# A decay check moved into the boot, a lag of four steps for the second matmuls, and a new order of preparation: an RWKV-6 and tanh-shrink kernel on one Trainium2 core

## The chip, the cores and the metric

The kernel runs on one core of a Trainium2 chip. The metric is the device time of one execution in microseconds; the time before is the median of three runs. The profile was taken from one further execution.

A core has engines that run side by side, each through its own list of instructions in order: TensorE (PE in the profile; its weight loads are PEld), VectorE (DVE), ScalarE (ACT), GpSimd (POOL) and SyncE (SP), which here only starts transfers. An instruction waits for semaphores that others raise. While it waits, all that stands behind it on the same engine waits too. This includes transfers: a transfer that may not yet overwrite its target holds up every later transfer of that queue.

## What is computed

Two layers, one after the other. The first is a linear recurrence (RWKV-6) over 768 tokens, for 4 batches and 8 heads of 48 channels; the second is a dense layer pair with the function h - tanh(h) in between.

```
for t in range(S):
    cur   = einsum(u * k[t], v[t])                  # outer product
    y[t]  = einsum(r[t], state + cur)
    state = w[t] * state + einsum(k[t], v[t])
x = y as (B*S, H*D)                                 # 3072 x 384
h = x @ w_in                                        # 384 -> 2048
out = (h - tanh(h)) @ w_out                         # 2048 -> 384
```

All is float32 on the chip, apart from the two weight matrices, which arrive in 64 bit and are turned into float32 there.

## The kernel before

**Blocks and steps.** The 3072 tokens are cut into 8 blocks of 384 (4 batches, 2 halves `q`). A block's dense part runs in 16 steps `f`, one for each 128 of the 2048 hidden channels. In a step `first` computes `hp`, the first product (3 matmuls of 128x384, six records in the profile, L629); ScalarE copies it to `h` (L632); VectorE and ScalarE make s = h*h (L643), qa (L645), hs and gT (both L635), a short polynomial in place of h - tanh(h), good for small h. Then `Second.add` adds gT times w_out to three accumulators in PSUM (`acc`, L676, again six records). `hp` has a single PSUM buffer, so the next hp waits for the copy to h. The tile `s` of step f is made in step f; qa, hs and gT of step f stand one step later in the program (`rest`). The second matmuls of step f come LAG steps after its hp; LAG is 3, and the pool of gT tiles has LAG + 1 buffers.

**The next block's attention between the steps.** While block i runs its 16 steps, the attention of block i + 1 is made in between, by the plan of `plan(i)`: `before` names what VectorE and ScalarE prepare in step f, `phases` what PE does, `ahead` what is begun for block i + 2, and `loads` which transfer is asked for. The pieces, for pairs of heads (`h1` = pairs 2 and 3, `h2` = pairs 0 and 1, in chunks of 64 tokens):

- `behind`: a scan from the right over the decays w, product of the decays after each token, into the tile `post` (L300, 128x780). `inverse`: the whole product of each chunk and its reciprocal, into `start` (L321, L323). `before`: the scan from the left into `pre` (L289). Both scans read the tile `w`.
- `times_behind`: post = k * post (L314). `times_before`: pre = r * pre (L307). `times_u`: k = u * k on ScalarE (L328).
- `turn`: transposes of post on PE (L386) and a copy `ks` (L388). `update`: k v products (L405) and the states of the chunks (L417, L428), which stay in SBUF.
- `own` and `earlier`: two products of a chunk with itself on PE (L363), taken into the tile `scores` under a mask on VectorE (L370).
- `from_states` (L469) and `from_scores` (L486): the result, copied into xT and `late` by ScalarE (L519). x has 384 rows in three tiles xT; each pair of heads leaves two holes of 16 rows in its tile, filled from the tile `late` by six small transfers (`fill_holes`, L526).
- `bound`: one ScalarE instruction (L334) that sums relu(w - 1) over the block's decays into `excess`, a check that no decay is above 1. At the very end all checks are counted, and if one fails, all is computed again by another path; with this input none fails.

The tiles w, k, r, post, pre and v_sb have one buffer each. So the load of block i + 2's w, asked for while block i runs, may start only when the last reader of block i + 1's w is done.

**The order is written out by hand.** PE, VectorE, ScalarE and SyncE run in program order. A load of the plan is tied by `begin_behind` to the ScalarE instruction that makes h in that step. Within a step the program has, in this order: hp and h, s, the rest of the step before, the weight conversion for step f + 2 (`extra`), the pieces of `before`, the phase, `ahead`, the load, the second matmuls of the lagging step, and, where the phase is "result 1", the "result 2" with its copies and hole fills.

**The boot.** Before block 0's steps, `boot` makes block 0's attention alone, with PE, VectorE and ScalarE waiting on each other, starts the weight loads and converts the first weights. Conversion of one step's weights (`convert`) takes three ScalarE instructions (L205, L208, L209) and two VectorE instructions (L212, L213) over 1536 columns in all. During block 0 the remaining weights are converted as well (step f makes those for f + 3). Only block 0 has this work.

For block 0 the plan has `w` of block 2 in step 11, `k` in 12, `r` in 13, "result 1" in 13 and `bound` of block 1 in 14.

Of the kernel before, what the change touches and what calls it, by code (L numbers as in the profile page):

```python
# [37 lines left out]
F32 = mybir.dt.float32  # L38
# [3 lines left out]
BF16 = mybir.dt.bfloat16  # L42
# [3 lines left out]
AF = mybir.ActivationFunctionType  # L46
# [5 lines left out]
P = 128  # L52
L = 64
NB = 384
NQ = S // NB
NCH = NB // L
NCP = NCH // 2
NPAIR = H // 2
# [12 lines left out]
BANK = 512  # L71
AHEAD = 6
RAWS = 5
LAG = 3

# [21 lines left out]
def kernel(  # L97
# [86 lines left out]


    blocks_n = B * NQ
    n_whole, n_excess, n_top = blocks_n * NPAIR * NCH, blocks_n, blocks_n * NF
# [11 lines left out]
    def convert(f, raw, _, halves=False):  # L199


        lo, hi = raw[:, :, 0], raw[:, :, 1]
        a = w_sb[:, f, :].bitcast(I32)
        up = conv.tile([P, 2 * DM], I32, name="up", tag="up", bufs=4)
        nc.scalar.activation(out=a.bitcast(F32), in_=hi.bitcast(F32), func=AF.Copy, scale=HIGH_SCALE)  # L205
        low, high = (up.bitcast(t).rearrange("p (n two) -> p n two", two=2)[:, :, i]
                     for i, t in enumerate((U16, F16)))
        nc.scalar.activation(out=high, in_=hi.bitcast(F32), func=AF.Copy, scale=SIGN_SCALE)  # L208
        nc.scalar.activation(out=low, in_=lo.bitcast(U32), func=AF.Copy, scale=2.0 ** -29)  # L209

        def part(at):
            return [lambda: nc.vector.tensor_single_scalar(a[:, at], a[:, at], 3, op=ALU.logical_shift_left),  # L212
                    lambda: nc.vector.tensor_tensor(out=a[:, at], in0=a[:, at], in1=up[:, at], op=ALU.add)]  # L213
# [10 lines left out]
    class Block:  # L224
# [102 lines left out]
                t = self.tokens("k", p, 1)  # L327
                nc.scalar.activation(out=t, in_=t, func=AF.Copy, scale=u_sb[:, p:p + 1])  # L328

        def bound(self):  # L330

            i = self.b * NQ + self.q
            junk = work.tile([P, WIDE], BF16, name="junk", tag="junk", bufs=1)
            nc.scalar.activation(out=junk, in_=self.tile("w")[:, 0:WIDE], func=AF.Relu, bias=shift[:, 3:4],  # L334
                                 accum_out=excess[:, i:i + 1])

        def held(self, p0, n):
            i = (self.b * NQ + self.q) * NPAIR * NCH
# [136 lines left out]

        def from_scores(self, yp, slots, first, last):
            for n, slot in slots:
                for p in slot:
                    for c in range(NCP):
                        for h in range(2):  # L480
                            for par in range(2):
                                toks = slice(64 * par, 64 * par + 64)
                                e0 = 64 * (h ^ (p % 2))
                                f0 = p * D2 + h * D
                                n0 = (n * NCP + c) * L
                                nc.tensor.matmul(yp[p % 2][e0:e0 + D, par, n0:n0 + L],  # L486
                                                 lhsT=self.v[toks, c, f0:f0 + D],
                                                 rhs=A[toks, h, p, c, :],
                                                 start=(first and n == slots[0][0] and c == 0),
                                                 stop=(last and (n, c) == (slots[-1][0], NCP - 1)),  # L490
                                                 skip_group_check=True)
# [58 lines left out]
        def prepare(self, name):  # L550
            what, *half = name.split()
            p0, n = (int(half[0]), UP) if half else (0, NPAIR)
            getattr(self, what)(*(() if what == "bound" else (p0, n)))

        def totals(self, m, p0, n):
            cols = slice(p0 * NB, (p0 + n) * NB)
            tot = self.tile("w")[:, cols] if m == 1 else self.tots[m]
            t2 = tot.rearrange("d (n two) -> d n two", two=2)  # L560
            nxt = dense.tile([P, NB], F32, name="tot", bufs=3, tag={1: "h", 2: "s", 4: "qa"}.get(m, "tot"))
# [64 lines left out]
    def first(xT, f, ps):  # L626
        hp = ps.tile([P, NB], F32, name="hp", tag="hp")
        for kc in reversed(range(KC)):
            nc.tensor.matmul(hp, lhsT=w_in_sb[:, f, kc, :], rhs=xT[kc],  # L629
                             start=(kc == KC - 1), stop=(kc == 0))  # L630
        h = dense.tile([P, NB], F32, name="h", tag="h")
        return h, nc.scalar.activation(out=h, in_=hp, func=AF.Copy, scale=1.0 / UPSCALE)  # L632

    def product(out, in0, scalar, in1, op0):
# [50 lines left out]
    def plan(i):  # L685


        ahead = {13: ("behind 2", "inverse 2"), 14: ("behind 0", "inverse 0")}
        if i == 0:
            phases = {6: "turn", 8: "own", 9: "update", 11: "earlier", 13: "result 1"}  # L690
            before = {0: ("behind 0", "inverse 0"), 1: ("before 2",), 2: ("before 0",),
                      3: ("times_behind 2",), 4: ("times_behind 0", "times_u 2"),
                      5: ("times_before", "held", "times_u 0"), 14: ("bound",)}
            converted = range(READY, NF)
            loads = {f: "weights" for f in (0, 1, 2, 4, 5, 6, 7, 8, 9, 10)}
            loads.update({3: "v", 11: "w", 12: "k", 13: "r"})
        else:
            phases = {4: "turn", 5: "own", 6: "update", 8: "earlier", 10: "result 1"}
            before = {0: ("before 2",), 1: ("before 0",), 2: ("times_behind 2", "times_behind 0"),
                      3: ("times_before", "held", "times_u 2"), 4: ("times_u 0",), 7: ("bound",)}  # L700
# [21 lines left out]
    def boot(ps, blk, later):  # L722
        h1, h2 = HALVES
        for p0 in HALVES:
            for name in ("w", "k", "r"):
                blk.load(name, p0, UP)
        blk.load_v()
        for _ in range(3):
            more_weights(nc.sync)
        ready = []  # L730

        def converted():
            for op in ready.pop(0):
                op()

        both = (h1, h1 + 1), (h2, h2 + 1)

        def decays(p0):
            blk.behind(p0, UP)
            blk.inverse(p0, UP)  # L740
            blk.times_behind(p0, UP)
            blk.times_u(p0, UP)
            blk.turn(ps, p0)
            return blk.before(p0, UP)

        decays(h1)
        own = blk.own(ps, h1)
        blk.times_before(h1, UP)
        earlier = blk.earlier(ps, h1)
        blk.bound()  # L750
        ins = decays(h2)
        begin_behind(ins, later.load("w"))
        own()
        blk.update_1(ps)
        blk.times_before(h2, UP)
        earlier()
        ready.append(convert(*raws.pop(0), halves=True))
        blk.results(ps)
        blk.result("from_scores", both[0])
        blk.update_2()  # L760
        blk.result("from_states", ALL, cs=(0, 1), more=True)
        own = blk.own(ps, h2)
        blk.result("from_states", ALL, cs=(2,))
        own()
        earlier = blk.earlier(ps, h2)
        earlier()
        ready.append(convert(*raws.pop(0)))
        blk.result_out(both[0], True)
# [141 lines left out]
```

## Time and profile before

| | |
|---|---|
| time, median of 3 runs | 620.99 us (620.25 to 622.24) |
| profiled span | 617.5 us |
| PE busy | 585.7 us, 95% |
| PE weight loads busy | 362.7 us, 59% |
| VectorE busy | 378.3 us, 61% |
| ScalarE busy | 235.6 us, 38% |
| boot, until the first hp | 28.11 us |
| one middle block, 16 steps | 72.1 us |
| `bound`, each of 8 | 1583 ns, and 190 ns to read its sum |
| transfers | 43.03 MB, mean 70 GB/s |

The page cuts the span into 40 slices of 15.4 us; a digit is the busy share of a slice in tenths. The chain of waits follows the work that ended last back to what released it, piece by piece with start and length. A row of a group or of the timeline has start, length, engine, line, operation, output and inputs, shapes, count, and in brackets how long the engine had been idle and what ended that. A queue of an engine (SPq) is its sequencer, which starts the transfers.

### The profile page before, as it was taken

The page shows a single profiled execution, that of the slowest core. Times are in us where ns is not written, and L with a number is a line of the kernel's source. Part 1 is how long each engine was busy: PE and PEld are TensorE (multiplying, and loading weights), DVE is VectorE, ACT ScalarE, POOL GpSimd, SP SyncE. Part 2 cuts the span into 40 slices and gives each one's busy share as a digit, 9 for nine tenths or more (in the row PEclk, how much of TensorE's full clock was granted, in tenths as well). Part 3 has the DMA queues.
Part 4 walks back from the last instruction along what each step waited for, and adds up shares of the span by engine and source line. Part 5 has one row for each costly group of instructions (what it writes and reads, how often), then busy time and mean ns, then how long its engine had stood idle before and what let it go on. Part 6 is the DMA issues. An engine that isn't in the chain of part 4 may idle for free.

```text
span 617.5 us, 12779 instructions
## 1 busy us (share of the span) xinstructions
PE 585.7 (95%) x5410; PEld 362.7 (59%) x5410; DVE 378.3 (61%) x777; ACT 235.6 (38%) x428; POOL 9.9 (2%) x39
## 2 busy tenths in 40 slices
PE   3779996999999999999999999999999999999996
PEld 3535663566655666566655666556665666555553
DVE  8899992766368553776457663685537764444442
ACT  3789773242224333242233422243332522332221
POOL 5000000000000000000000000000000000000000
PEclk9999999899999999999999999999999999999999
DMA  8594414111212032020321112120320200001001
GB/s 313 169 373 154 155 54 164 40 37 54 63 52 78 1 103 63 1 77 2 105 62 38 39 54 63 51 77 1 104 63 1 76 2 2 11 0 40 0 0 41
DMA packets 23420, 43.03 MB, mean 70 GB/s; under 512 B 2112, under 2 KB 21312, under 8 KB 23360
## 3 DMA queue, kind: packets, MB, share of 16 engines
q1 hardware_dynamic: 22944, 41.89, 20.3%
q8 instruction: 43, 0.70, 0.5%
q10 hardware_dynamic: 352, 0.25, 0.1%
q14 instruction: 17, 0.14, 0.1%
q0 software_dynamic: 64, 0.05, 0.0%
HBM read 36.28 MB, written 4.72 MB: 66 GB/s over the span
## 4 chain that ended last, share of the span: by engine, by line
PE 89%; DVE 6%; issue 1%; DMA 1%; POOL 1%; ACT 0%; SPq 0%; PEld 0%; PEldq 0%; DVEq 0%; POOLq 0%
PE acc L676 39%; PE hp L629 39%; PE att L363 4%; PE att L469 2%; PE att L486 2%; PE att L405 2%; PE att L386 1%; DVE pre L289 1%; DMA xT<-late 1%; DVE w_sb L213 1%; DVE post L300 1%; POOL mask_all L144 1%; DVE scores L370 0%; DVE gT L635 0%; DVE w_sb L212 0%
## 5 line engine op out<-in xcount | busy, mean ns | idle before, releaser
L629 PE MATMUL hp<-xT,w_sb 128*128 128x384 f32 x768 | 273.7, 493 | 13.0 <-DMA xT<-late 6.4
L676 PE MATMUL acc<-w_sb,gT 128*128 128x384 f32 x768 | 271.5, 490 | 0.8
L629 PEld LDWEIGHTS hp<-xT,w_sb 128*128 128x128 f32 x768 | 146.2, 192 | 117.0 <-issue 14.1
L676 PEld LDWEIGHTS acc<-w_sb,gT 128*128 128x128 f32 x768 | 143.3, 190 | 95.7 <-issue 2.5
L643 DVE CUSTOM_DVE_ANT_0 s<-h 128x384 f32<-128x384 f32 x128 | 71.1, 556 | 193.5 <-ACT h L632 193.2
L632 ACT ACTIVATE h<-hp 128x384 f32<-128x384 f32 x128 | 62.8, 491 | 322.3 <-issue 288.5
L635 DVE SCALAR_TENSOR_TENSOR gT<-qa,hs 128x384 f32<-128x384 f32 x128 | 71.5, 558 | 16.7 <-PE acc L676 0.5
L645 ACT ACTIVATE qa<-s,shift 128x384 f32<-128x384 f32 x128 | 77.6, 606 | 5.6 <-DVE top L643 5.4
L635 DVE SCALAR_TENSOR_TENSOR hs<-h,s 128x384 f32<-128x384 f32 x128 | 70.9, 554 | 0.0
L300 DVE TENSOR_TENSOR_SCAN post<-w,seed 128x780 f32<-128x780 f32 x16 | 28.5, 1784 | 10.9 <-DMA w<-in_wT 10.9
L370 DVE COPY_PREDICATED scores<-mask_all,att 128x768 f32<-128x768 uint8 x32 | 30.6, 1004 | 0.8 <-PE att L363 0.6
L289 DVE TENSOR_TENSOR_SCAN pre<-w,start 128x780 f32<-128x780 f32 x16 | 28.5, 1784 | 0.0
L386 PE MATMUL att<-ident,post 128*128 128x128 f32 x96 | 13.4, 292 | 10.0 <-DVE post L314 10.0
L328 ACT ACTIVATE k<-k,u_sb 128x384 f32<-128x384 f32 x32 | 17.7, 604 | 7.5 <-DVE post L314 7.5
L386 PEld LDWEIGHTS att<-ident,post 128*128 128x128 f32 x96 | 11.9, 151 | 12.4 <-DVE post L314 10.2
L208 ACT ACTIVATE up<-raw 128x768 f16<-128x768 f32 x16 | 17.0, 1066 | 0.0
L209 ACT ACTIVATE up<-raw 128x768 uint16<-128x768 uint32 x16 | 16.8, 1050 | 0.0
L519 ACT COPY late<-att 128x384 f32<-128x384 f32 (+1 forms) x9 | 4.3, 478 | 31.5 <-PE att L486 30.5
L213 DVE CUSTOM_DVE_ANT_0 w_sb<-w_sb,up 128x1536 uint16<-128x1536 uint16 (+1 forms) x17 | 15.5, 911 | 0.8
L428 DVE TENSOR_TENSOR states<-states,att 128x192 f32<-128x192 f32 x40 | 14.2, 354 | 2.2
L363 PEld LDWEIGHTS att<-r,k 48*64 48x64 f32 x768 | 12.7, 140 | 4.7 <-issue 4.4
L405 PEld LDWEIGHTS att<-v_sb,ks 64*64 64x64 f32 x704 | 12.8, 143 | 4.2 <-issue 3.8
(52 smaller groups left out, 255.6 us busy)
## 6 DMA issues: line engine op xcount, KB each, us to landing
raw<-in_weights SPq DMA_DIRECT2D x16, 768.0 KB, 5.5
w<-in_wT SPq DMA_DIRECT2D x7, 780.0 KB, 4.6
k<-in_kT SPq DMA_DIRECT2D x7, 768.0 KB, 5.6
r<-in_rT SPq DMA_DIRECT2D x7, 768.0 KB, 4.7
v_sb<-in_v SPq DMA_DIRECT2D x8, 576.0 KB, 3.9
out_y<-o SPq DMA_DIRECT2D x23, 192.0 KB, 1.9
xT<-late SPq DMA_DIRECT2D x44, 24.0 KB, 1.9
w<-in_wT SPq DMA_DIRECT2D x2, 390.0 KB, 4.8
```

The source lines that it names most:

```text
L289: return nc.vector.tensor_tensor_scan(out=self.tile("pre")[:, cols], data0=self.tile("w")[:, cols], data1=start[:, cols], initial=0.0, op0 ...
L300: return nc.vector.tensor_tensor_scan(out=back(t[:, 0:width]), data0=back(self.tile("w")[:, a:a + width]), data1=back(seed[:, a:a + width] ...
L363: nc.tensor.matmul(dst, lhsT=self.chunk(lhs, p, 2 * c + par)[rows], rhs=src, start=True, stop=True)
L370: return lambda: nc.vector.copy_predicated(out=A[:, :, p0:p0 + UP].rearrange("s h p c t -> s h (p c) t"), mask=mask.to_broadcast([P, 2, UP ...
L386: nc.tensor.transpose(tp[:, p, c * P:(c + 1) * P], self.chunk("post", p0 + p, 2 * c, n=2), ident)
L405: nc.tensor.matmul(kvp[64 * h:64 * h + 64, par, n0:n0 + D], lhsT=ks[toks, p % UP, c, 64 * h:64 * h + 64], rhs=self.v[toks, c, e0:e0 + D], ...
L629: nc.tensor.matmul(hp, lhsT=w_in_sb[:, f, kc, :], rhs=xT[kc], start=(kc == KC - 1), stop=(kc == 0))
L632: return h, nc.scalar.activation(out=h, in_=hp, func=AF.Copy, scale=1.0 / UPSCALE)
L635: return lambda: nc.vector.scalar_tensor_tensor(out=out, in0=in0, scalar=scalar, in1=in1, op0=op0, op1=ALU.mult)
L643: nc.vector.tensor_tensor_reduce(out=s, in0=h, in1=h, scale=1.0, scalar=0.0, op0=ALU.mult, op1=ALU.max, accum_out=top[:, n:n + 1])
L645: return g, [lambda: nc.scalar.activation(out=qa, in_=s, func=AF.Square, bias=shift[:, 4:5]), product(hs, h, TOP, s, ALU.mult), product(g, ...
L676: nc.tensor.matmul(acc, lhsT=g[:, j * P:(j + 1) * P], rhs=w_out_sb[:, f, :], start=(f == 0), stop=(f == NF - 1))
```

## The change

Four things, all in the order of work; no arithmetic changes.

1. `bound` now runs for half of the heads at a time (`excess` has two columns per block). Block 1's two halves move from step 14 of block 0 into the boot; the blocks after run both in step 7 as before.
2. LAG is 4: gT has five buffers, h has four, and each step's second matmuls come one step later.
3. Block 0's steps prepare block 1 in another order: the left scans, needed only by "earlier" in step 11, move to steps 4 and 6, the products with k move forward to 1 and 2, "turn" from 6 to 5.
4. In the boot the left scan of h1 comes ahead of the product with k, `own` of h2 is computed and masked ahead of the state updates, `earlier` of h2 stands between two parts of `from_states`, and `from_scores` goes through a pair of heads in reverse, as the copies after it do.

The aim is to have the tile w free before block 2's load is asked for, to take work that is not yet needed out of the stretch in which VectorE is behind, and to fill waits of the boot.

```
-LAG = 3
+LAG = 4
...
-        def bound(self):
-            i = self.b * NQ + self.q
-            junk = work.tile([P, WIDE], BF16, ...)
-            nc.scalar.activation(out=junk, in_=self.tile("w")[:, 0:WIDE], ...)
+        def bound(self, p0):
+            i = 2 * (self.b * NQ + self.q) + p0 // UP
+            junk = work.tile([P, UP * NCH * LP], BF16, ...)
+            nc.scalar.activation(out=junk, in_=self.tile("w")[:, p0 * NCH * LP:(p0 + UP) * NCH * LP], ...)
...
         def from_scores(self, yp, slots, first, last):
             for n, slot in slots:
-                for p in slot:
+                for p in reversed(slot):
...
-        h = dense.tile([P, NB], F32, name="h", tag="h")
+        h = dense.tile([P, NB], F32, name="h", tag="h", bufs=4)
...
         if i == 0:
-            phases = {6: "turn", 8: "own", 9: "update", 11: "earlier", 13: "result 1"}
-            before = {0: ("behind 0", "inverse 0"), 1: ("before 2",), 2: ("before 0",),
-                      3: ("times_behind 2",), 4: ("times_behind 0", "times_u 2"),
-                      5: ("times_before", "held", "times_u 0"), 14: ("bound",)}
+            phases = {5: "turn", 8: "own", 9: "update", 11: "earlier", 13: "result 1"}
+            before = {0: ("behind 0", "inverse 0"), 1: ("times_behind 2",), 2: ("times_behind 0",),
+                      4: ("before 2",), 5: ("times_u 2",), 6: ("before 0", "times_u 0"),
+                      7: ("times_before", "held")}
...
     def boot(ps, blk, later):
-        decays(h1)            # behind, inverse, times_behind, times_u, turn, before
+        blk.behind(h1, UP)
+        blk.inverse(h1, UP)
+        blk.before(h1, UP)
+        blk.times_behind(h1, UP)
+        blk.times_u(h1, UP)
+        blk.turn(ps, h1)
         own = blk.own(ps, h1)
         blk.times_before(h1, UP)
         earlier = blk.earlier(ps, h1)
-        blk.bound()
-        ins = decays(h2)
+        blk.bound(h1)
+        blk.bound(h2)
+        ...                   # behind, inverse, times_behind, times_u, turn of h2
+        ins = blk.before(h2, UP)
         begin_behind(ins, later.load("w"))
         own()
-        blk.update_1(ps)
+        own = blk.own(ps, h2)
         blk.times_before(h2, UP)
         earlier()
+        blk.update_1(ps)
+        own()
         ready.append(convert(*raws.pop(0), halves=True))
         blk.results(ps)
         blk.result("from_scores", both[0])
         blk.update_2()
+        ready.append(convert(*raws.pop(0)))
+        later.bound(h1)
         blk.result("from_states", ALL, cs=(0, 1), more=True)
-        own = blk.own(ps, h2)
+        earlier = blk.earlier(ps, h2)
         blk.result("from_states", ALL, cs=(2,))
-        own()
-        earlier = blk.earlier(ps, h2)
         earlier()
-        ready.append(convert(*raws.pop(0)))
         blk.result_out(both[0], True)
+        later.bound(h2)
         blk.fill_holes([nc.sync, nc.scalar, nc.gpsimd])
```

More of the change, by code (lines that the diff above doesn't have):

```diff
@@ L186 @@
     blocks_n = B * NQ
-    n_whole, n_excess, n_top = blocks_n * NPAIR * NCH, blocks_n, blocks_n * NF
+    n_whole, n_excess, n_top = blocks_n * NPAIR * NCH, 2 * blocks_n, blocks_n * NF
     holds = const.tile([P, n_whole + n_excess + n_top], F32, name="holds", tag="holds")
@@ L328, in times_u @@
                 nc.scalar.activation(out=t, in_=t, func=AF.Copy, scale=u_sb[:, p:p + 1])
-        def bound(self):
-            i = self.b * NQ + self.q
-            junk = work.tile([P, WIDE], BF16, name="junk", tag="junk", bufs=1)
-            nc.scalar.activation(out=junk, in_=self.tile("w")[:, 0:WIDE], func=AF.Relu, bias=shift[:, 3:4],
-                                 accum_out=excess[:, i:i + 1])
+        def bound(self, p0):
+            i = 2 * (self.b * NQ + self.q) + p0 // UP
+            junk = work.tile([P, UP * NCH * LP], BF16, name="junk", tag="junk", bufs=1)
+            nc.scalar.activation(out=junk, in_=self.tile("w")[:, p0 * NCH * LP:(p0 + UP) * NCH * LP], func=AF.Relu,
+                                 bias=shift[:, 3:4], accum_out=excess[:, i:i + 1])
         def held(self, p0, n):
@@ L552, in prepare @@
             p0, n = (int(half[0]), UP) if half else (0, NPAIR)
-            getattr(self, what)(*(() if what == "bound" else (p0, n)))
+            getattr(self, what)(*((p0,) if what == "bound" else (p0, n)))
         def totals(self, m, p0, n):
@@ L560, in totals @@
             t2 = tot.rearrange("d (n two) -> d n two", two=2)
-            nxt = dense.tile([P, NB], F32, name="tot", bufs=3, tag={1: "h", 2: "s", 4: "qa"}.get(m, "tot"))
+            nxt = dense.tile([P, NB], F32, name="tot", bufs=4 if m == 1 else 3, tag={1: "h", 2: "s", 4: "qa"}.get(m, "tot"))
             nxt = nxt[:, 0:n * NB // (2 * m)]
@@ L699, in plan @@
             before = {0: ("before 2",), 1: ("before 0",), 2: ("times_behind 2", "times_behind 0"),
-                      3: ("times_before", "held", "times_u 2"), 4: ("times_u 0",), 7: ("bound",)}
+                      3: ("times_before", "held", "times_u 2"), 4: ("times_u 0",), 7: ("bound 2", "bound 0")}
             converted = ()
@@ L736, in boot @@
         both = (h1, h1 + 1), (h2, h2 + 1)
[L738 to L744, printed above, removed]
-        decays(h1)
+        blk.behind(h1, UP)
[4 more added lines that the diff above has]
+        blk.turn(ps, h1)
         own = blk.own(ps, h1)
@@ L749, in boot @@
         earlier = blk.earlier(ps, h1)
-        blk.bound()
-        ins = decays(h2)
+        blk.bound(h1)
+        blk.bound(h2)
+        blk.behind(h2, UP)
+        blk.inverse(h2, UP)
+        blk.times_behind(h2, UP)
+        blk.times_u(h2, UP)
+        blk.turn(ps, h2)
+        ins = blk.before(h2, UP)
         begin_behind(ins, later.load("w"))
         own()
-        blk.update_1(ps)
+        own = blk.own(ps, h2)
         blk.times_before(h2, UP)
         earlier()
+        blk.update_1(ps)
+        own()
         ready.append(convert(*raws.pop(0), halves=True))
```

## The prediction

> **What bounds the kernel now.** First the slices of the page.
>
> ```profile
> PE   3779996999999999999999999999999999999996
> ...
> DVE  8899992766368553776457663685537764444442
> ...
> PEclk9999999899999999999999999999999999999999
> ```
>
> PE is full except in slices 1 to 3 (to 46 us), in slice 7 (93 to 108 us) and in the last. The only dip of the clock is beside the dip in slice 7. Then the busy time by stage: stretch, length, and busy us of PE, PEld, DVE, ACT, POOL with instruction counts, then granted clock, DMA share and GB/s.
>
> ```profile
> 28.10:49.50 21.40, 16.43 (x42) 8.34 (x43) 20.63 (x36) 18.17 (x25) 0.00 (x0) 0.92 0.87 315
> 49.50:102.60 53.10, 52.95 (x608) 33.12 (x608) 40.52 (x79) 39.28 (x59) 0.13 (x2) 1.00 0.32 111
> 102.60:115.20 12.60, 6.27 (x13) 3.61 (x14) 8.53 (x18) 1.61 (x3) 0.00 (x0) 0.73 0.45 158
> 115.20:187.30 72.10, 71.99 (x686) 44.70 (x685) 43.48 (x91) 23.77 (x47) 0.13 (x2) 1.00 0.17 53
> ```
>
> From 28 to 49.5 VectorE is the bound (20.63 of 21.40 us). From 49.5 PE is, without a gap, and from 115.2 every block takes 72.10 us with 71.99 of PE: nothing there to win. What is left is the boot (28 us), the VectorE stretch, and a hole at the change from block 0 to block 1. The chain of waits says what makes the hole.
>
> ```profile
> 96.78 1.08 PE acc L676 x4
> 97.85 1.58 ACT junk L334 x2
> ...
> 99.45 0.38 SPq L274
> ...
> 100.99 0.80 SPq L526
> 101.78 0.04 issue
> 101.83 6.97 DMA xT<-late
> 108.80 0.14 issue
> 108.93 4.18 PE hp L629 x6
> 113.11 2.11 PE acc L676 x6
> ```
>
> SyncE's queue runs in order. The w load of block 2 (plan step 11) must overwrite the tile that `bound` of block 1 (step 14, L334) still reads. So w, k and r, and behind them the six hole fills (L526), start only when `bound` ends. The list of waits of that queue has the size:
>
> ```profile
> SPq L274 <- ACT junk L334: 22.5, 1, 22.5
> ```
>
> The fills need only the copies of block 1's result, which began at 94.72, yet they go out from 100.99, behind 2.3 MB. PE ends its last matmul at 102.58 and waits until 108.93, 6.35 us; the six matmul records of the next hp then take 4.18 us, where they take 1.94 elsewhere.
>
> **What the Trainium skill says.** "TensorE: Matmul & The Clock Gate", Part 1: after an idle window of about 3.4 us the PE clock is halved until it has been busy about as long. The trace agrees: 6.35 us idle, then 4.18 for 1.94. "DMA: Bandwidth & Descriptors", Issuing engines are not separate DMA queues: all transfers share the same 16 engines. The trace agrees: the fills beside the loads took up to 7.6 us to land, 1.8 to 1.9 elsewhere. "ScalarE: Activation LUTs", What ACT_TABLE_LOAD costs: with a pointer bias 280 ns + 0.833 ns per column, for 1560 columns an estimate of 1.58 us; the trace has 1583 ns.
>
> **The change, part by part.**
>
> *1. `bound` of block 1 into the boot.* The remaining readers of block 1's w tile are the scans; the last ("before 0") now stands at step 6, about 59 us. The w load then goes at step 11 (h at 79.88), k at 12, r at 13 (89.37), each by its own trigger, apart by 4 to 5 us, about their median time to land (4.6 to 5.6). When the copies come at 94.72 the queue is empty. Six fills take 3.98 us to issue (4.08 in the next block) and 1.9 to land: 95.2 + 4.0 + 1.9 = 101.1, before PE asks at 102.6, and xT[2], asked first, is filled first. So 6.35 us of waiting and 4.18 - 1.94 = 2.24 of slow clock go: **-8.6**. All of it is on PE's path, since PE is full before and after. VectorE's own wait for w (10.9 us ahead of L300) goes too, hidden by the lag.
>
> *2. `bound` in two halves.* Per half the price above gives 0.93 us for 780 columns, plus the 0.19 of the accumulator read. In blocks 2 to 7 that adds some 0.5 us to ScalarE, which is busy 23.8 of 72.1: nothing.
>
> *3. Preparation by need.* Between w_sb[3] (ends 39.8) and w_sb[5] VectorE gives up two L289 scans (next start 1.69 us later) and takes two L314 products (0.86): 0.83 us earlier for w_sb[4], 1.66 for w_sb[5]. These are what hp waits for:
>
> ```profile
> 44.55 1.78 DVE L289 TENSOR_TENSOR_SCAN pre<-w,start 128x780 f32<-128x780 f32 x1
> ...
> 44.78 2.17 PE L629 MATMUL hp<-xT,w_sb 128*128 128x384 f32 x6 [0.64 <-DVE w_sb L213]
> ...
> 49.52 2.17 PE L629 MATMUL hp<-xT,w_sb 128*128 128x384 f32 x6 [0.64 <-DVE w_sb L213]
> ```
>
> *4. The lag of four.* It puts every hp one acc group (1.94 us) earlier in PE's order, so while PE waits for weights it has less to do meanwhile. With 3: hp[4] at 44.78 - 0.83 = 43.95. Behind it only acc[0], then hp[5] at 43.95 + 2.01 + 1.94 = 47.90, when w_sb[5] is just there (49.52 - 1.66 = 47.86). From there PE is full, but one acc group is still owed that the old order had behind it: 47.90 + 1.94 = 49.84 against 49.52, less 0.07 of restart: **+0.25**. The two parts nearly cancel.
>
> Does PE stay full to step 16? Times on the old clock. ScalarE at steps 5 and 6 does 5.92 and 4.56 us (h, qa, three conversions, k times u, ks) while PE does 5.2 and 3.9: h[7] ends near 60.95, and hp[8], which needs its PSUM buffer, is due at 60.9, a tie. VectorE has w_sb[12] (behind the eleven state updates, 4.3 us) at 81.45, hp[12] is due at 81.65, slack 0.2. Other weights have 0.9 us or more. I take 0 to 0.5 lost, middle 0.1. The extra gT and h buffers only make the lag possible.
>
> *5. The boot.* VectorE: the L289 scan ahead of the first L314 product fills the 0.49 us for which that waited on GpSimd. The mask of own(h2) ahead of the state updates takes away the 0.65 us before the last mask. With the small waits beside them, placing each row after the one before it has the last mask done at 23.85, not 25.36. But ScalarE does not keep up. earlier(h2) now stands ahead of from_states of pair 2 on PE, where its PSUM buffer comes free only with the fourth state update, so the result copies start at 23.4 (23.14 before), and last 1.96 us to 25.35. Then `bound` of the later block's second half (0.93 + 0.19, less overlap: 1.0) is queued ahead of the two xT copies: 26.4 against 26.47 before. Behind those are VectorE's xT copies (each waits for ScalarE's) and then hp[0]: about 28.0 against 28.11. The reversed from_scores lets the first copy go half a group (0.45 us) sooner, hidden by that `bound`. Bounds: 0 (ScalarE as worked out) and 1.6 (0.49 + 0.65 + 0.45, if it does not bind). I take **-0.1**: the copies and `bound` are one after the other on one engine, with durations from rows.
>
> *6. Blocks 1 to 7 and the end.* PE order shifts, its sum does not. At the end four acc groups are left, not three; two still stand between the last hp and the check, the same 0.51 us of PE waiting there: nothing.
>
> Sum: -8.6 + 0.25 + 0.1 - 0.1 = -8.35, so 620.99 - 8.35 = **612.6 us**.
>
> **The rivals.**
> *A, the boot pays too* (0.10): the half `bound` fits beside the copies, and the 1.6 comes through: 611.1. For it: VectorE's queue holds two waits that the order removes. Against: the ScalarE sum above.
> *B, a new stall follows the lag* (0.12): hp[12] or hp[8] is late by 0.5 us more, or the gap ahead of hp[4] (about 1.75 us, with no acc group behind hp[3] now) halves the clock for one group, 2.24: 612.6 + 2.7 = 615.3. For it: slack of 0.2 us. Against: a gap of 2.3 us ahead of hp[3] left the clock full.
> *C, the fills stay late* (0.05): r, asked for at step 13, is still moving at 95, and six small fills creep beside it; half the hole stays, clock included: 617.
> *D, slower* (0.03): w is held by something else that is as late (the trace shows only the last releaser), so the hole stays whole; the lag's loss of 0.25 and one slow group of 2.24 come on top: 620.99 + 0.25 + 2.24 = 623.5. Against: no other reader of that tile stands later than step 6.
> The forecast itself: 0.70.
>
> **How the numbers follow.** The time is that of the forecast. Low end 610.3: A less the spread of the measured runs (0.75 below their median). High end 615.6: B, with 0.3 for measuring. Outside lie C, D and the tails of A and B, some 0.16. Faster by over 0.3% (below 619.1): forecast, A, B, C, 0.95 with a little taken off for causes not seen; within: 0.02; slower: 0.03.
>
> **What would show it.** In the chain after the change, block 1's first hp follows an acc group with no DMA piece, and the six records take 1.94 or so, with the clock at full in slice 7. The fills land in about 2 us. The w load of step 11 waits for h, not for L334. The first hp starts near 28, the idle ahead of hp[5] is gone, the idle ahead of hp[4] grows to about 1.75. I am wrong if a wait for xT or for w_sb appears on PE after 48 us, if ScalarE's L334 does not stand between the copies of the boot, or if a block from 115 on takes other than 72.1 us.

## The result, and the profile after

The changed kernel takes **614.81 us** (median of 4 runs, 614.09 to 615.3) against 620.62 us (4 runs, 619.19 to 622.24) for the kernel before: a ratio of 0.9905, 95% interval 0.9877 to 0.9932. Run again later beside eleven runs of before it took 614.47 us, ratio 0.9882 (0.9858 to 0.9906). So it is 6 to 7 us faster. The forecast was 612.6 us: the direction and the cause hold, and some 2 us of the gain are missing. Executions of one kernel differ by up to 3.5 us (e1 below: 611.04 to 614.55), so a profile, which shows one of them, can lie that far from a median.

The slices of the page after, the same three rows as before:

```profile
PE   3669899999999999999999999999999999999996
...
DVE  8798986855377644766367563786447663444442
...
PEclk9999899999999999999999999999999999999999
```

The hole of slice 7 is gone, and the dip of the clock with it. In its place there is an 8 in slice 5 (61 to 77 us), in PE and in PEclk. Busy time by stage, after (stretch, length, busy us of PE, PEld, DVE, ACT, POOL with counts, clock, DMA share, GB/s):

```profile
28.76:49.07 20.31, 14.42 (x37) 7.05 (x37) 19.08 (x36) 17.06 (x25) 0.00 (x0) 0.92 0.87 327
49.07:98.00 48.93, 47.24 (x586) 29.70 (x586) 44.02 (x81) 36.10 (x53) 0.13 (x2) 0.97 0.47 162
98.00:111.50 13.50, 13.50 (x43) 7.99 (x42) 8.59 (x18) 4.06 (x9) 0.00 (x0) 1.00 0.05 13
111.50:183.60 72.10, 71.99 (x685) 44.73 (x684) 43.63 (x91) 24.03 (x49) 0.13 (x2) 1.00 0.17 53
```

The change from block 0 to block 1 (third row) is solid: 13.50 of 13.50 us. A later block takes 72.10 us with 71.99 of PE, to the digit what it took before. But the second row has lost 1.69 us of PE time and runs at a clock of 0.97, where before it had 52.95 of 53.10 at 1.00. The chain of waits over the change of block has no transfer in it any more (start, length, what); block 1's first hp is the piece at 105.66:

```profile
97.72 2.13 PE hp L629 x6
99.86 1.94 PE acc L676 x6
101.79 1.94 PE hp L629 x6
103.73 1.94 PE acc L676 x6
105.66 1.94 PE hp L629 x6
```

SyncE's queue in that stretch, after: w, k and r wait for h only, no longer for `bound`; the fills go out at 98.34.

```profile
SPq L274 <- ACT h L632: 12.1, 3, 5.2
```

Where the second row lost its time is in PE's timeline, after (start, length, engine, line, what, idle time and releaser in brackets):

```profile
41.18 2.17 PE L629 MATMUL hp<-xT,w_sb 128*128 128x384 f32 x6 [2.73 <-DVE w_sb L213]
45.12 2.17 PE L629 MATMUL hp<-xT,w_sb 128*128 128x384 f32 x6 [1.77 <-DVE w_sb L213]
...
49.07 2.17 PE L629 MATMUL hp<-xT,w_sb 128*128 128x384 f32 x6
...
67.99 2.10 PE L629 MATMUL hp<-xT,w_sb 128*128 128x384 f32 x6
71.63 1.61 PE L405 MATMUL att<-v_sb,ks 64*64 64x48 f32 x80 [1.55 <-DVE scores L370]
73.17 3.90 PE L676 MATMUL acc<-w_sb,gT 128*128 128x384 f32 x6
```

The rows at 45.12 and 49.07 are as forecast (1.77 us of idle ahead of hp[4], none ahead of hp[5]). The last two are new: `update` waits 1.55 us for the masks of `own`, and the acc group behind it runs at half speed, 3.90 us for the 2.2 that it takes elsewhere. `update` writes its products into the scratch tiles of PSUM (pool ps_a, two buffers), and those two hold the two `own` products until VectorE has masked them into `scores`. VectorE's row of that masking, after and then before:

```profile
70.56 1.94 DVE L370 COPY_PREDICATED scores<-mask_all,att 128x768 f32<-128x768 uint8 x2
```

```profile
68.52 1.91 DVE L370 COPY_PREDICATED scores<-mask_all,att 128x768 f32<-128x768 uint8 x2
```

Before, the masks came 2 us sooner (0.65 us of that because the first hp did, 28.11 against 28.76) and `update` ran without a wait behind the hp of 68.22. VectorE does the same 69 instructions between the boot and the masks in both orders, 42.4 us of work, without a break of note before. After, it stands idle for 0.61 us in a weight conversion and for 0.98 us at step 6: there it is ahead of ScalarE, which has the copies of `turn` (L388) to do before it makes h. ScalarE and VectorE, after:

```profile
55.81 1.48 ACT L388 COPY ks<-att 128x768 f32<-128x768 f32 x2
57.18 0.51 ACT L632 ACTIVATE h<-hp 128x384 f32<-128x384 f32 x1
```

```profile
57.72 0.56 DVE L643 CUSTOM_DVE_ANT_0 s<-h 128x384 f32<-128x384 f32 x1 [0.98 <-ACT h L632]
```

The second left scan (60.83) and the product with r (65.60) are still ahead of the masks at that time.

The difference of the two profiled spans, 617.5 - 613.6 = 3.9 us, is less than that of the medians, because the profiled execution of before (619.19 us) was one of its shortest: its other executions in this study had spans of up to 622.4 us, mostly around 619.

### The profile page after: what moved, and what is told of

It reads as the page before. It is cut to its first block, busy times and chain, and to the rows that moved or that the text cites. A ratio compares the mean times of both kernels' runs of the same rounds, so it can differ in the third digit from the quotient of the medians.

```text
span 613.6 us, 12671 instructions
## 1 busy us (share of the span) xinstructions
PE 584.2 (95%) x5410; PEld 361.6 (59%) x5410; DVE 378.2 (62%) x777; ACT 237.5 (39%) x444; POOL 11.4 (2%) x39
## 4 chain that ended last, share of the span: by engine, by line
PE 87%; DVE 6%; ACT 2%; issue 1%; POOL 1%; PEld 0%; ACTq 0%; PEldq 0%; DVEq 0%; POOLq 0%
PE acc L676 39%; PE hp L629 38%; PE att L363 3%; PE att L469 2%; PE att L405 2%; PE att L486 2%; PE att L386 1%; DVE w_sb L213 1%; POOL mask_all L144 1%; DVE post L300 1%; DVE gT L635 1%; DVE w_sb L212 1%; DVE pre L289 1%; DVE s L643 1%; DVE hs L635 1%
## 5 line engine op out<-in xcount | busy, mean ns | idle before, releaser
L405 PE MATMUL att<-v_sb,ks 64*64 64x48 f32 x704 | 13.4, 220 | 2.6 <-DVE scores L370 2.2
```

Source lines behind the costliest of these rows:

```text
L405: nc.tensor.matmul(kvp[64 * h:64 * h + 64, par, n0:n0 + D], lhsT=ks[toks, p % UP, c, 64 * h:64 * h + 64], rhs=self.v[toks, c, e0:e0 + D], ...
```

## The experiments

In what follows "the pass" is `bound` of block 1, and "order by need" the new order of preparation. There were twelve runs, e8 and e11 repeats among them, each in rounds with the kernel before on the same chip. The median of before differs between the chips by up to 0.6 us (620.72 to 621.35), so the ratios are what is to be compared; e1 to e4 shared a chip, e5 to e8 another, e9 to e11 a third, and e12 had one of its own.

| kernel | median us | ratio to before, 95% |
|---|---|---|
| pass at step 9, nothing else (e1) | 612.14 | 0.9871 (0.9851 to 0.9892) |
| the same again (e11) | 611.86 | 0.9854 (0.9836 to 0.9873) |
| the change, pass back at step 14 (e2) | 623.92 | 1.0049 (1.0032 to 1.0066) |
| the change with lag 3 (e3) | 611.56 | 0.9856 (0.9842 to 0.987) |
| the change, update at step 10 (e4) | 615.57 | 0.9915 (0.9901 to 0.9928) |
| the change, pass at step 9 (e5) | 613.99 | 0.9884 (0.9859 to 0.9909) |
| e5 with the boot of before (e6) | 613.85 | 0.9879 (0.9855 to 0.9903) |
| e5 with lag 3, a left scan and the product with r later (e7) | 612.33 | 0.9853 (0.9825 to 0.988) |
| the change again (e8) | 614.47 | 0.9882 (0.9858 to 0.9906) |
| before, hole fills from ScalarE's queue (e9) | 620.16 | 0.9992 (0.998 to 1.0004) |
| e6 with lag 3 (e10) | 611.87 | 0.9857 (0.9839 to 0.9876) |
| e1 with lag 4, halves (e12) | 613.49 | 0.987 (0.9854 to 0.9887) |

### Is the hole the whole gain? e1, e11 and e2

e1, on the kernel before:

```
-                      5: ("times_before", "held", "times_u 0"), 14: ("bound",)}
+                      5: ("times_before", "held", "times_u 0"), 9: ("bound",)}
```

> The kernel before with one edit: bound of block 1, whole, at step 9 of block 0 instead of step 14; boot, lag and order of preparation as before. Theory (the gain is the hole at the change from block 0 to block 1, and the other three parts together cost some 2.5 to 4 us): the wait for xT and the slow hp after it go, -8.6 us, so about 612.0, some 3 us under the changed kernel; first hp at 28.1 and no wait of PE between 49.5 and 102.6. Rival (the other parts carry a share of the gain, or hide what the early load collides with): 615 or more, with a wait left on PE before step 16 or for xT.

Measured: 612.14 us, ratio 0.9871, and 611.86, 0.9854 on another chip. One moved name takes away 8.0 to 9.1 us (0.0129 and 0.0146 of 621); the medians say 8.7 and 8.9. In e1's profile SyncE's queue sends w at 81.00, k at 86.63, r at 90.50 and the fills from 96.22, and PE runs on through the change of block:

```profile
101.09 2.10 PE L676 MATMUL acc<-w_sb,gT 128*128 128x384 f32 x6
103.02 2.10 PE L629 MATMUL hp<-xT,w_sb 128*128 128x384 f32 x6
```

> The kernel before with the pass over block 1's decays whole at step 9 instead of step 14, run again on the chip of the two others, as their yardstick: 611.0 to 612.5 us by the theory; 614 us or more if its first time was luck of the chip's clock.

e2, the other side, on the changed kernel:

```
-                      7: ("times_before", "held")}
+                      7: ("times_before", "held"), 14: ("bound 2", "bound 0")}
...
-        later.bound(h1)
-        later.bound(h2)
```

> The changed kernel with block 1's two bound halves back at step 14 of block 0, out of the boot. Theory: the hole is back in full, 6.4 us idle and 2.2 of slow clock, less about 1.0 us that the boot gains because no bound stands between its copies: 614.8 + 8.6 - 1.0 = 622.4. Rival (lag, order and boot have a gain of their own): 620 or less.

Measured: 623.92 us, ratio 1.0049. The hole is back, as PE's timeline of this kernel shows:

```profile
110.82 3.54 PE L629 MATMUL hp<-xT,w_sb 128*128 128x384 f32 x5 [6.51 <-DMA xT<-late]
```

The time is 1.5 us above the 622.4 expected: the 1.0 us that the boot was to gain did not show. So the earlier pass is the whole gain, and **the rest of the change costs 3.0 us** (0.0049 of 621; 2.0 to 4.1 by the interval). Both together fit the changed kernel: 0.9854 to 0.9871 times 1.0049 is 0.990 to 0.992, measured 0.9905 and 0.9882.

### Is the queue's order the whole of the hole? e9

```
-                self.fill_holes([nc.sync])
+                self.fill_holes([nc.scalar if self.b + self.q == 1 and self.b == 0 else nc.sync])
```

> The kernel before, with one edit: the six fills of block 1's decay inputs, which stand behind the wait for the w load on SyncE's queue, are issued from ScalarE's queue instead. The pass over the decays stays at step 14. Theory (the queue's order made the hole, and the pass itself is still a chain of its own): the fills go out near 95 us and the 6.5 us wait ahead of block 1's first preparation product goes, but VectorE still waits some 10 us for w, until about 104, so that its masks come late and TensorE waits some 3 us at a later update or accumulation: 615.5 to 617.5 us. Rival (the lag of three steps hides VectorE's wait, the hole was the queue's order alone): 612 to 613 us, no wait of TensorE above 1 us between 90 and 115. Second rival (the fills were held by the bound itself, not by the queue): 620 to 621 us, the hole stays.

(The six fills are not decay inputs: they fill the holes of x, for block 1's first hp.) Measured: 620.16 us, ratio 0.9992: no gain that can be told. That is the time which the second rival named, but not for its reason: the fills did go early and landed in 1.9 us, and block 1's first hp came at 104.21 without a wait. PE waited at other places instead. ScalarE, VectorE and PE in this kernel:

```profile
96.42 3.17 ACTq L526 DMA_DIRECT2D xT<-late  x5
```

```profile
106.94 1.78 DVE L300 TENSOR_TENSOR_SCAN post<-w,seed 128x780 f32<-128x780 f32 x1 [13.59 <-DMA w<-in_wT]
```

```profile
100.24 2.20 PE L629 MATMUL hp<-xT,w_sb 128*128 128x384 f32 x6 [1.27 <-ACT h L632]
...
104.21 2.10 PE L629 MATMUL hp<-xT,w_sb 128*128 128x384 f32 x6
110.82 4.21 PE L676 MATMUL acc<-w_sb,gT 128*128 128x384 f32 x6 [4.51 <-DVE gT L635]
```

Issuing the fills holds ScalarE's queue for 3.17 us, so that h and with it `bound` come later; w comes later still, and VectorE stands before its scan for 13.59 us with s, hs and gT of the dense part behind it in the queue. PE waits 1.27 us for h and 4.51 for gT, and the slow clock after that takes 2.1 more: 7.9 us together, nearly the 8.6 of the hole. The wait behind the wait is there, as the first theory said, but its size was under-estimated (615.5 to 617.5 expected), in part since the cost of issuing on ScalarE was left out: w went out at 102.29, before at 99.45. What helps is to let w go early, not to take the fills past it.

### Which part of the rest costs? e3, e5, e6, e8

e3 changes one number, `LAG = 4` to `LAG = 3`.

> The changed kernel with the lag of the second matmuls at 3 again, all else as changed. Theory: one acc group (1.94 us) fits into the wait ahead of hp[4] (1.8 us) instead of being owed later; all that comes after stands at the same times, the wait of the update for the masks included: 614.8 - 1.9 = 612.9. Rival (the lag of 4 is needed, since gT comes too late for 3 in the new order): 614.8 or more, with a wait of acc for gT on PE.

Measured: 611.56 us, ratio 0.9856, against 0.9905 and 0.9882 of the changed kernel. The acc group fills the gap ahead of hp[4] (no wait there), the wait of 1.56 us at `update` stays, and the acc group behind it took 2.20 us here.

e5 moves the pass out of the boot, to step 9 (`9: ("bound 2", "bound 0")` in place of the two calls in `boot`); e6 moreover puts the whole `boot` of before back.

> The changed kernel with block 1's two bound halves at step 9 of block 0 and none of them in the boot. Theory (the boot's loss against the forecast is not the bound; the stretch of waits on PE without a releaser and the old jitter are): first hp 0.3 to 0.5 us sooner, the copies now waiting for PE: 614.8 - 0.4 = 614.4; the load of w still goes at step 11, no hole. Rival (bound in the boot is what cost the 0.65): 613.8 or less, first hp at 27.9 or before.

> The kernel of the previous experiment (bound at step 9) with the boot of the kernel before. Theory (the boot's new order wins nothing): within 0.7 us of that experiment, first hp within 0.5 us of its first hp, and VectorE's wait of 0.6 us between the two instructions of w_sb[2] (it is in all four kernels with the new boot and in neither with the old one) goes: 613.8 to 614.4. Rival (the new boot is worth the 1.5 us that VectorE's rows show): 615.5 or more, first hp 1 us later.

Measured: 613.99 and 613.85 us, ratios 0.9884 and 0.9879, beside 614.47 and 0.9882 of the changed kernel on the same chip:

> The changed kernel itself once more. Theory (the slow acc group of 3.90 us behind the update is an event of single executions): 614.3 to 615.3 in the median, and a profile with the wait of 1.55 us but the acc group either at 2.20 or at 3.9. If it is at 3.9 again, the slow clock belongs to this order of work, and the 3.25 us that lag 3 gained are 1.94 of the lag and 1.3 of the clock.

The three can't be told apart: the new order of the boot is worth nothing that these runs can tell, and whether the early pass stands in the boot or in step 9 makes no difference either. In e8's profile the wait of 1.53 us at `update` is there again, and the acc group behind it took 2.20 us; hp[3] (3.03) and hp[4] (4.18) were slow instead. So the slow group behind `update` is an event of single executions, as the theory had it.

### Lag and order of preparation, each for itself: e10 and e12

With the boot of before and the pass at step 9, all four combinations of lag and order were run. Three of them, e6, e10 and e12, keep the pass in two halves and the reversed `from_scores`; e11 has neither, so that lag and order are not quite all that differs from it. e10 is e6 with `LAG = 3`; e12 is e6 with block 0's plan of before:

```
-            phases = {5: "turn", 8: "own", 9: "update", 11: "earlier", 13: "result 1"}
+            phases = {6: "turn", 8: "own", 9: "update", 11: "earlier", 13: "result 1"}
...
-            before = {0: ("behind 0", "inverse 0"), 1: ("times_behind 2",), 2: ("times_behind 0",),
-                      4: ("before 2",), 5: ("times_u 2",), 6: ("before 0", "times_u 0"),
-                      7: ("times_before", "held"), 9: ("bound 2", "bound 0")}
+            before = {0: ("behind 0", "inverse 0"), 1: ("before 2",), 2: ("before 0",),
+                      3: ("times_behind 2",), 4: ("times_behind 0", "times_u 2"),
+                      5: ("times_before", "held", "times_u 0"), 9: ("bound 2", "bound 0")}
```

> The changed kernel with the boot of before, the pass over block 1's decays whole at step 9, and the second matmuls lagging three steps: of the change only the earlier pass and the preparation by need are left. Theory (the lag of four steps costs about 2 us, the order of the preparation nets nothing): 613.85 less 1.9 to 2.5, so 611.3 to 612.0 us, the same as the pass alone within 0.7 us. Rival (the order by need is worth its 1.7 us once lag and boot are out of the way): 610.5 us or less.

> The kernel before with the pass over block 1's decays at step 9 and the second matmuls lagging four steps; the boot and block 0's order of preparation are those of before. With e1 (lag 3, old order, 611.9), e10 (lag 3, new order, 611.9) and e6 (lag 4, new order, 613.85) it fills the square of lag and order. Theory (the lag moves one accumulation, 1.94 us, out of the stretch in which TensorE waits for weights, and the order of preparation nets nothing at either lag, because the later waits take back what the weights gain): the waits ahead of hp[4] and hp[5] at 0.4 + 1.94 and 0.6, no wait at the update, 613.3 to 614.3 us. Rival (the order by need is what makes a lag of four bearable, as the prediction had it with its 1.66 us): 615.0 to 615.8 us.

| | order of before | order by need |
|---|---|---|
| lag 3 | 611.86 us, 0.9854 (e11) | 611.87 us, 0.9857 (e10) |
| lag 4 | 613.49 us, 0.987 (e12) | 613.85 us, 0.9879 (e6) |

Across: the order nets nothing at lag 3 (the medians differ by 0.01 us) and, by the ratios, a loss of 0.6 us at lag 4, inside the intervals. Down: the lag costs 1.0 us (0.0016) and 1.4 us (0.0022) by the ratios, 1.6 and 2.0 us by the medians. The intervals of the ratios overlap in both columns; what supports a cost of the lag is that the times of the two kernels of a column do not overlap (611.61 to 612.2 and 612.79 to 613.56; 611.6 to 612.15 and 613.38 to 614.29; on different chips, it is true), and that e3 beside e8 and the changed kernel has the same sign. In e12 the wait ahead of hp[4] was 2.58 us, as expected, but the slow clock came there too (3.76 us for 2.17) and covered the wait at hp[5], so a share of the cost may be the clock's. The profiles say why the order nets nothing. PE's timeline of e10, with the order by need:

```profile
43.06 2.10 PE L676 MATMUL acc<-w_sb,gT 128*128 128x384 f32 x6
45.00 2.10 PE L629 MATMUL hp<-xT,w_sb 128*128 128x384 f32 x6
46.94 2.10 PE L676 MATMUL acc<-w_sb,gT 128*128 128x384 f32 x6
48.87 2.10 PE L629 MATMUL hp<-xT,w_sb 128*128 128x384 f32 x6
...
71.41 1.61 PE L405 MATMUL att<-v_sb,ks 64*64 64x48 f32 x80 [1.53 <-DVE scores L370]
```

and of e11, with the order of before:

```profile
43.92 2.10 PE L676 MATMUL acc<-w_sb,gT 128*128 128x384 f32 x6
46.39 2.17 PE L629 MATMUL hp<-xT,w_sb 128*128 128x384 f32 x6 [0.38 <-DVE w_sb L213]
48.40 2.10 PE L676 MATMUL acc<-w_sb,gT 128*128 128x384 f32 x6
51.14 2.17 PE L629 MATMUL hp<-xT,w_sb 128*128 128x384 f32 x6 [0.64 <-DVE w_sb L213]
...
71.86 1.61 PE L405 MATMUL att<-v_sb,ks 64*64 64x48 f32 x80
```

The waits for weights at hp[4] and hp[5] do go: counted from the first hp (27.95 in e10, 28.81 in e11), hp[5] comes 1.4 us sooner. But what VectorE was spared there it still has to do ahead of the masks, at steps 4 to 7, and it does not keep the time: in e10 it stands 1.08 us for h at step 6, where in e11 it does not wait. Counted from the first hp, PE is at hp[9] 1.2 us sooner and the masks come 1.0 us later, so `update` waits 1.53 us. That wait is in every profile with the new order as it stands (1.53 to 1.56 us), also at lag 3, and in none with the old one, also at lag 4.

### Can the new wait be taken away? e4 and e7

e4: `9: "update"` to `10: "update"` in the changed kernel. e7: e3 with the pass at step 9, and `"before 0", "times_before", "held"` moved to step 9 as well.

> The changed kernel with the update phase of block 1 at step 10 instead of 9 in block 0's plan. Theory: the 1.55 us for which PE's update waits for the two own masks (its PSUM buffers) go, and with them the slow clock of the acc group behind (3.90 for 1.94): 614.8 - 3.5 = 611.3. Rival (PE waits for VectorE's backlog anyway, only at another place): a wait of similar length for a weight or for the states at steps 10 to 13, 613.5 to 615.

> The changed kernel with lag 3, bound at step 9, and the second left scan and the product with r at step 9 too, behind the own masks (not at 6 and 7). Theory: the masks come 3.5 us sooner, the update's wait of 1.56 us on PE goes, about 0.5 of it comes back ahead of hp[12] or of earlier, since VectorE has no slack left by then: lag 3 alone 611.6, less 1.0, less 0.4 of the boot = 610.2. Rival (VectorE's backlog only moves the wait, as it did with the update at 10): 611.2 or more, with a wait of 1.5 us at steps 11 or 12.

Measured: 615.57 us (0.9915) and 612.33 us (0.9853). In the profiles of both the wait at `update` is gone and another has come, at `earlier`, which needs a scratch tile that the state updates hold. PE's timeline of e4, then of e7:

```profile
82.96 1.69 PE L363 MATMUL att<-pre,post 48*64 48x64 f32 x96 [2.30 <-DVE states L428]
```

```profile
82.02 1.69 PE L363 MATMUL att<-pre,post 48*64 48x64 f32 x96 [1.13 <-DVE states L428]
...
86.34 2.17 PE L629 MATMUL hp<-xT,w_sb 128*128 128x384 f32 x6 [0.49 <-DVE w_sb L213]
```

The rival was right both times about the wait. Two things blur the sizes. In e4's profile the first hp came only at 30.10 us, after 1.97 us of waiting for a fill of the boot, which the edit does not touch. In e7's profile the clock was slow at hp[3] (3.14 us) and in the group behind it; that execution took 613.50 us, the other three 611.95 to 612.52. In the profile after VectorE is busy 44.02 of the 48.93 us up to 98 us, and in both tries a wait for it was put elsewhere, not removed; that no order removes it is not shown. By their ratios e3, e7, e10 and e11 (0.9853 to 0.9857) can't be told apart, and the interval of e1 overlaps theirs. Their medians are 2.1 to 3.3 us below those of the changed kernel; e1 needs one moved name for it.

## Why the prediction was right or wrong, point by point

- **1, the hole, -8.6: right.** The pass alone gave 8.0 to 9.1 us, putting it back took 9 to 10 us. The fills took 4.44 us to issue (3.98 was used) and landed in 2.2 us at the median, still before PE asked. One clause of that step failed: that VectorE's wait for w was "hidden by the lag". e9 shows that, with the fills early, it holds PE at gT for 4.51 us. Before, it cost nothing only because PE stood in the hole meanwhile.
- **2, two halves: right.** The halves took 940 and 946 ns and their reads 187 and 208 (0.93 and 0.19 were used). In the middle block ScalarE went from 23.77 to 24.03 us, and the block stayed at 72.10.
- **3 and 4, +0.25: the first half right, the sum wrong.** The idle ahead of hp[4] is 1.77 us (about 1.75 forecast) and hp[5] does not wait. hp[0] to hp[4] took 16.36 us where 15.84 was worked out; the 0.52 between them are covered by a wait of 0.61 us inside the third weight conversion, for which the trace names no cause (last section).
- **The step that failed** is "PE stays full to step 16", with 0 to 0.5 and 0.1 taken. It looked at the buffer of hp and at the weights, and there its two tight places held: 0.2 us of waiting at hp[8] in e2 and e6, none at hp[12]. It left out the two scratch tiles of the attention products: `update` needs the tiles that the masks read. The order puts no more work ahead of the masks than before. But PE, without its waits for weights, is at hp[9] 39.23 us after the first hp instead of 40.11, and the masks come 41.80 us after it instead of 40.41, since VectorE loses again what it was spared in front: 0.61 us in the conversion and 0.98 at step 6. The step had counted ScalarE's work at steps 5 and 6 for the buffer of hp, and not for VectorE, which waits for the same h. The term measures **1.55 us** instead of 0.1. With it the -1.66 of step 3 is given back, and what is left of the pair is the bare cost of the lag, 1 to 2 us. None of the prediction's own signs of being wrong came; it had none for this wait.
- **The slow clock** was in rival B as one group, 2.24 us, behind the gap ahead of hp[4]. It comes, but not always there: behind `update` in the profile after (3.90 for 2.20, 1.7 us), at hp[3] and hp[4] in e8. By size that was about right, by place only in e8, and there hp[3] was slow too.
- **5, the boot, -0.1: no gain, as forecast, but not as worked out.** e8, e5 and e6 (the new boot with the pass in it, without it, and the old boot) can't be told apart. ScalarE's second half of the pass stood between the copies as worked out (26.11 to 27.15), and the scan did fill VectorE's wait for GpSimd: L307 starts at 9.96 us, before at 10.41. But VectorE's last mask was done at 24.70, not at 23.85, and ScalarE's copies began at 24.13, not at 23.4, behind products `from_states` ahead of which PE waits 1.03 us for nothing that the profile shows (last section). The first hp came at 28.76 in the profile after (28.0 forecast) and at 28.49 to 30.10 in the others with this boot (e3, e4, e8); without the pass in the boot at 27.83 to 28.51 (e2, e5, e7), with the old boot at 27.95 to 28.81. These ranges overlap, so single profiles say little of it.
- **6, the end: right.** PE's wait for the count is 0.5 us in both lists of waits.

Put together: 612.6, plus 1.45 for the wait at `update`, is 614.05; up to 1.7 for a slow group in some of the executions leads to the 614.5 to 614.8 measured. Profile against profile the terms can be laid side by side: 617.5 - 8.35 = 609.15 us of span would have been the forecast, and 613.6 came. Of these 4.45 us, 1.45 are the wait at `update`, 1.70 the slow group behind it, 0.76 the later first hp and 0.52 the stretch to hp[4], 4.43 in all. The medians show only some 2 us of it, because the profile of before was of a short execution, and that of the changed kernel of a long one. That 614.8 lies inside the stated 610.3 to 615.6 is in part luck: the high end was rival B's, set for another stall.

Rival B had the sum (615.3) and the form, a new stall; but it put it down to the lag, and the stall belongs to the order of preparation: it stands at lag 3 with the new order (e3, e10) and not at lag 4 with the old one (e12). A, C and D did not come: the boot paid nothing, and the fills went out with an empty queue.

## What to carry to other kernels

When an instruction that only reads a buffer holds back a load, look at what stands behind that load in its queue: here a check of 1.6 us cost 8 to 9 us, and moving it was all that was needed. When work is moved later on an engine that is busy through nearly the whole stretch, walk through every buffer which that engine frees, scratch tiles of PSUM too, and not only through the data that the next engine reads; a wait that is removed in front may come back behind. And when a bundle of edits gives less than the sum, run its largest part alone: here that was faster than the bundle by 2 to 3 us in the medians.

## What the runs showed of the hardware

**GpSimd stands still beside a VectorE scan.** GpSimd's rows in the boot, before:

```profile
7.31 0.22 POOL L144 TENSOR_SCALAR_AFFINE_SELECT mask_all<-mask_all 64x32 int8<-64x32 int8 x1
7.48 0.12 POOL L295 MEMSET post<- 128x1 f32 x2
```

and after, with VectorE's rows of the same time below:

```profile
7.30 1.70 POOL L144 TENSOR_SCALAR_AFFINE_SELECT mask_all<-mask_all 64x32 int8<-64x32 int8 x1
8.96 0.12 POOL L295 MEMSET post<- 128x1 f32 x2
```

```profile
7.15 1.83 DVE L289 TENSOR_TENSOR_SCAN pre<-w,start 128x780 f32<-128x780 f32 x1
9.08 0.96 DVE L314 TENSOR_TENSOR post<-k,post 128x768 f32<-128x768 f32 x1
```

The scan starts at 7.15 and ends at 8.98; the select, which GpSimd begins at 7.30, then takes until 9.00, and the memset behind it until 9.08. L314, which in the kernel before waited for that memset until 7.60, starts at 9.08 here. VectorE lost little by it, since the scan filled the time. The Trainium skill has this, in "SBUF — State Buffer", SBUF: two separate sides: a VectorE instruction with two SBUF inputs, against a GpSimd instruction that reads SBUF, holds the port pair that the two share for its whole length. The trace agrees (1.70 us for 0.22), and so do the others: 1.70 us in all seven profiles with the new boot, 0.22 or 0.23 in all seven with the old. The prediction did not use it.

**The clock was halved behind shorter gaps than 3.4 us, and not behind each.** In the profile after the granted clock was 0.55 from 73.2 to 77 us, behind an idle time of 1.55 us and the 80 small products of `update` (1.61 us, at full clock), while 2.73 us ahead of hp[3] left the next group at 2.17. In e12 an idle time of 2.25 us left hp[3] at 2.17 us, and 2.58 us ahead of hp[4] made it 3.76. "TensorE: Matmul & The Clock Gate", Part 1, says that the window of about 3.4 us runs freely, and that where a kernel falls in it varies from run to run; the wandering agrees with that, the length of the idle time does not. What decides it within a gap stays open.

**Two waits without a releaser.** VectorE, third weight conversion, after:

```profile
34.42 0.96 DVE L213 CUSTOM_DVE_ANT_0 w_sb<-w_sb,up 128x1536 uint16<-128x1536 uint16 x1 [0.61 <-DVE w_sb L212]
```

It is 0.60 to 0.61 us in the profiles with the new boot, and absent with the old. PE, too, waits 1.03 us at 21.45 in the boot, ahead of products `from_states`, where the list of waits names nothing: 0.55 to 1.39 us in the profiles with the new boot. With the old boot there is one of at most 0.74 us, ahead of products `own`. Neither was isolated.
